# A convolution with a gated two-layer product in fp32: taps' homes, the rounds of four sums, and the engine of the weight sums

## The chip, the core and the metric

One core of a Trainium2 chip runs the whole program. The core has five engines that work side by side, each through its own queue in order: TensorE (PE, matrix products, with PEld for the loads of its weights), VectorE (DVE), ScalarE (ACT), GpSimd (POOL) and SyncE (SP, which issues DMAs). DMAs are also issued from GpSimd's queue, among them those that add to what lies at their target ("accumulating"). The metric is the device time of one execution in microseconds (us).

## The reference

Eight sequences of 4096 tokens with 192 channels pass a causal convolution of 7 taps. Its weights are a softmax over the taps, one set for each of 8 groups of channels. The result is multiplied with w_in (192 x 2048), goes through the gate h / (1 + exp(-1.702 h)), and is multiplied with w_out (2048 x 192). All in fp32.

```python
w = np.exp(weight - np.max(weight, axis=-1, keepdims=True))
w = w / (np.sum(w, axis=-1, keepdims=True) + 1e-09)
out = np.einsum('hk,bskhg->bshg', w, x_unf)      # 7 taps, causal
x = out.reshape(B * S, D)
h = x @ w_in
g = h * (1.0 / (1.0 + np.exp(-1.702 * h)))
return g @ w_out
```

## The kernel before

**Steps.** The 32768 tokens are worked in 32 steps ("big") of two parts n of 512 tokens. Step 0 (`first_step`, `second_first`) also loads the weights and makes all that later steps use. Steps 1 to 31 each have a hidden stage (`hidden`, product with w_in and the gate) and an output stage (`second`, product with w_out and the store).

**Fewer products by sums.** Both products are done with fewer matrix products than the plain way, at the price of sums of blocks. In the hidden stage 41 products (`TERMS`) of a weight block with a data block replace 48. Weight blocks 0 to 11 are w_in's own, the others are sums of these (`SUMS_W`, two sets v, in the tile `w_in_s`), made once, in step 0. Data blocks 0 to 5 are the convolution's own (`own`), 6 to 19 are sums of them: `SUMS_H`, `SUMS_M`, `SUMS_F`, `SUMS_L` and others, made for every step one step ahead. Each data block also needs its halves crossed to the other 64 partitions (`cross`, small DMAs on SP's queue, or copies of ScalarE where an engine is given). Products go to PSUM banks p0 to p3. The list `HIDDEN` says in which order the products (`mm`), the copies of banks to SBUF (`copy`, "a" is ScalarE and "v" VectorE), the `join`s of partial results on VectorE and the gates (`gelu`, ScalarE) are issued. The places k0 to k8 of copies are in `KS`: k0 is row 1 of the tile `room`, k7 and k8 are the halves of `osbs`.

**The output stage** follows the list `PLAN`. Its 78 rounds (`go`) are each one product of three small matmuls and a fourth beside them. Its operands lie in "spots": spots 0 and 1 are the two halves of `osbs`, spots 2 to 4 rows 1 to 3 of `room`, and spots 5 to 20 the blocks of `g`, the gate's output, which are also summed in place (`sum` on VectorE, `acc` by accumulating DMAs from GpSimd's queue). `osbs` has a second use: near the end of the stage results are transposed into it (`turn`; half n = 0 is spot 0, half n = 1 spot 1) and stored from it, so that it is the store's buffer.

**The convolution of later steps** runs beside both. The channels are three blocks c of 64. For steps from 3 on, ScalarE makes each tap k: it multiplies the shifted x with the tap's weight into a "home" (`tap`, `tap_home`, places in `TAP_SPOTS` and `TAP_HALVES`; a pair (i, k) there is spot i, from column block k on). Taps of blocks 0 and 1 are then added by accumulating DMAs in the order of `LATER`: under the key (c, k) stand triples (block, target, source), which are issued after tap k of block c; target 0 is the convolution's own place. Taps of block 2 are added by GpSimd (L575). There are 21 taps a step, in the order block 1, 0, 2; 18 are issued in `PLAN` and the last three, taps 4 to 6 of block 2, in the next hidden stage. `piece` issues the next of the sums `SUMS_M` (GpSimd) and crossings of the next step; `late` ends them.

**The boundary between two stages.** A hidden stage begins with the products to p1, p2 and p3, with the tap (2, 4) on ScalarE between them, then ScalarE copies p1 to k0, and the fourth product goes to p1 again.

**Step 0's end and step 1.** `second_first` makes step 0's output by sums and products of larger blocks. Its last sums are p5 and q12 (VectorE, L1015 and L1038). GpSimd makes the weight sums of set 0 and nine sums of common blocks (`make_common_1`), VectorE those of set 1. SP's queue holds, in this order, crossings of sums that GpSimd makes, the load of x for step 3 (`load_x(3)` at the end of `first_step`), and the stores of step 0, which two entries of `after_copy` issue beside the first two copies of VectorE in step 1's hidden stage. The taps of block 1 for step 2 are VectorE's (`convs_next`, L554 and L556). For step 2 the taps of block 0 are added by a tree of accumulating DMAs (`TREE`), those of block 2 by GpSimd.

Of the kernel before, what the change touches and what calls it, by code (L numbers as in the profile page):

```python
# [15 lines left out]
def kernel(  # L16
# [29 lines left out]
    nc = tc.nc  # L46
# [5 lines left out]
    P = 128  # L52
# [106 lines left out]
    TAP_HALVES = {1: ((3, 0), (1, 0), (11, 0), (2, 0), (2, 2), (11, 2)), 2: ((11, 2), (13, 0), (16, 2), (15, 2), (11, 2), (13, 0)), 3: ((5, 0), (6, 0), (12, 2), (16, 2), (15, 2), (16, 0))}  # L159
# [39 lines left out]
    def own(big):  # L199
# [35 lines left out]
        ],  # L235
        [
# [9 lines left out]
            (15, 3), (10, 5), (12, 7), (2, 13), (5, 5), (17, 11), (8, 0), (18, 10), (14, 6), (9, 14), (7, 9), (4, 4),  # L246
            (6, 19), (11, 4), (1, 14), (16, 18), (19, 16), (13, 8), (20, 17), (0, 18),
        ],
        [
            (12, 12), (18, 3), (7, 15), (3, 10), (5, 11), (15, 1), (16, 4), (13, 7), (10, 9), (19, 6), (8, 2),  # L250
            (6, 0), (14, 8), (9, 10), (17, 2), (20, 11), (2, 6), (1, 3), (11, 1), (4, 9), (0, 0),
# [181 lines left out]
    def add_up(v, dst, a, op, b, eng=vec):  # L433
        if op == "+":
            eng.tensor_add(v(dst), v(a), v(b))  # L435
        elif op == "-":
            eng.tensor_sub(v(dst), v(a), v(b))  # L437
        elif op == "n" and eng is not vec:
            eng.tensor_add(v(dst), v(a), v(b))
            eng.tensor_scalar_mul(v(dst), v(dst), -1.0)  # L440
        elif op == "n":
            vec.scalar_tensor_tensor(
                out=v(dst), in0=v(a), scalar=-1.0, in1=v(b), op0=ALU.mult, op1=ALU.subtract
            )
        else:
            eng.tensor_scalar_mul(v(dst), v(a), -1.0)

    def sums_w_in(v, eng=vec):
        for item in SUMS_W[v]:
            add_up(lambda j: w_in_s[:, j, v * P : (v + 1) * P], *item, eng=eng)  # L450
# [66 lines left out]
    def transpose_x(big, c, n=None):  # L517
# [11 lines left out]
        h if isinstance(h, int) else spot(h[0])[:, h[1] : h[1] + 2, :] for h in ((5, 2), 6, (13, 0), 7, (6, 2), (13, 2))  # L529
# [19 lines left out]
    def conv(big, c, k, ns=slice(0, 2), times=vec.tensor_scalar_mul):  # L549
# [19 lines left out]
    def tap(big, c, k):  # L569
# [4 lines left out]
        if k and c not in DMA_TAPS and big > 1:  # L574
# [108 lines left out]
    def prepare(big):  # L683
# [9 lines left out]
        yield f"done {big}", 0.0, lambda: need(f"taps {big}")  # L693
# [753 lines left out]
```

## Time and profile before

| | us |
|---|---|
| median of 3 runs | 2339.22 (2339.06 to 2341.03) |
| the profiled execution | 2337.84 |
| its span in the trace | 2336.1 |

The profile's page gives the busy time of each engine. A row of a timeline has the start and the length in us, the engine, the line of the code, the operation, the tiles written and read, and in brackets the idle time before it with what ended it. A row of the windows has the stretch, its length, the busy time of PE, PEld, DVE, ACT and POOL with the number of instructions, then the granted share of TensorE's clock, the busy share of the DMA engines and GB/s. A row of DMA issues has the number, the size of each and the median time from issue to landing.

### The profile page before, as it was taken

Reading aid. Unit: us, or ns where it says so; the run is one execution under the profiler, and the core shown is the slowest. Engines: PE = TensorE matmul, PEld = TensorE weight load, DVE = VectorE, ACT = ScalarE, POOL = GpSimd, SP = SyncE. Lnnn points to the kernel's source line nnn. Section 1 sums busy time; section 2 is a strip of 40 time slices with the busy share of each in tenths; the row PEclk is TensorE's granted clock in tenths of the full one; section 3 lists DMA queues with packets and bytes.
Section 4 is the critical chain, followed back from the end, with each engine's and each line's share of the span. In section 5 each row is a group of like instructions: output and inputs, shape, how many; then the busy total and the mean of one; then the engine's idle time right before and its main releaser. Section 6 shows DMA issues by size and latency. Waiting matters only on the chain.

```text
span 2336.1 us, 64199 instructions
## 1 busy us (share of the span) xinstructions
PE 2290.0 (98%) x25090; PEld 1331.0 (57%) x25090; DVE 2161.6 (93%) x3023; ACT 1703.4 (73%) x3331; POOL 1117.9 (48%) x1257
## 2 busy tenths in 40 slices
PE   9979999999999999999999999999999999999999
PEld 5345655555555555555566555555565666555555
DVE  8968989999999998999899999999999999999998
ACT  8557767777777777777776777777777777777745
POOL 1844544545544455545455444555444554454510
PEclk9989999999999999999999999999999999999999
DMA  9768787787987788977879877889777888777743
GB/s 201 125 144 160 153 175 145 151 158 150 175 166 153 153 160 153 177 152 144 158 148 177 160 153 151 157 162 176 155 153 152 159 169 171 153 153 136 148 98 69
DMA packets 348557, 359.30 MB, mean 154 GB/s; under 512 B 131552, under 2 KB 269152, under 8 KB 348256
## 3 DMA queue, kind: packets, MB, share of 16 engines
q0 software_dynamic: 82192, 196.32, 47.9%
q1 hardware_dynamic: 264416, 158.50, 29.7%
q8 instruction: 199, 3.26, 0.6%
q14 instruction: 102, 0.84, 0.1%
q10 hardware_dynamic: 1648, 0.39, 0.1%
HBM read 53.15 MB, written 25.17 MB: 34 GB/s over the span
## 4 chain that ended last, share of the span: by engine, by line
PE 82%; DVE 6%; DMA 5%; POOL 3%; issue 2%; ACT 1%; SPq 1%; POOLq 0%; DVEq 0%; ACTq 0%
PE slot L707 33%; PE slot L1144 24%; PE sums L1144 13%; PE sums L707 12%; DVE g L437 1%; DMA osbs<-room 1%; DVE room L437 1%; POOL conv_t L437 1%; DVE room L435 1%; SPq L99 1%; DMA g<-in_moe_w_in_dram 1%; DMA xin<-in_x_dram 1%; DMA g<-g 1%; DMA w_form<-w_form 0%; DMA room<-g 0%
## 5 line engine op out<-in xcount | busy, mean ns | idle before, releaser
L707 PE MATMUL slot<-conv_t,w_in_s 64*128 64x512 f32 x3372 | 928.8, 592 | 6.3 <-DVE room L1038 4.9
L1144 PE MATMUL slot<-g,w_form 128*32 128x256 f32 x5872 | 728.1, 380 | 1.5 <-ACT room L1169 1.1
L707 PEld LDWEIGHTS slot<-conv_t,w_in_s 64*128 64x128 f32 x3372 | 444.6, 187 | 329.1 <-issue 252.4
L437 DVE TENSOR_TENSOR g<-g 128x1024 f32<-128x1024 f32 x372 | 447.5, 1230 | 17.0 <-ACT g L826 9.3
L707 PE MATMUL sums<-conv_t,w_in_s 64*128 64x512 f32 x1284 | 426.7, 595 | 16.1 <-ACT osbs L798 15.8
L1144 PEld LDWEIGHTS slot<-g,w_form 128*32 128x32 f32 x5872 | 367.3, 110 | 120.5 <-ACT room L1169 13.1
L1144 PE MATMUL sums<-g,w_form 128*32 128x256 f32 x3800 | 428.0, 379 | 1.5 <-ACT sums L1173 1.5
L437 POOL TENSOR_TENSOR conv_t<-conv_t 128x256 f32<-128x256 f32 x310 | 273.9, 957 | 220.1 <-PE slot L707 85.6
L819 ACT ACTIVATE g<-slot 128x512 f32<-128x512 f32 x494 | 265.9, 625 | 131.9 <-PE slot L707 124.5
L573 ACT ACTIVATE g<-xt,cw 128x512 f32<-128x512 f32 x418 | 292.9, 727 | 82.5 <-DVE g L437 45.5
L1120 POOL DMA_DIRECT2D g<-g x124 | 118.3, 954 | 445.7 <-PE slot L1144 220.1
L1144 PE MATMUL slot<-g,w_out_s 128*32 128x256 f32 x4080 | 324.4, 382 | 4.3 <-DVE room L435 3.8
L575 POOL TENSOR_TENSOR conv_t<-conv_t,g 128x512 f32<-128x512 f32 x180 | 293.1, 1628 | 54.6 <-ACT g L573 52.1
L1169 ACT COPY room<-slot 32x256 f32<-32x256 f32 x434 | 158.3, 365 | 181.8 <-PE slot L1144 166.8
L1144 PEld LDWEIGHTS sums<-g,w_form 128*32 128x32 f32 x3800 | 217.5, 110 | 83.0 <-ACT room L1169 5.7
L707 PEld LDWEIGHTS sums<-conv_t,w_in_s 64*128 64x128 f32 x1284 | 181.2, 188 | 137.6 <-issue 94.3
L1144 PEld LDWEIGHTS slot<-g,w_out_s 128*32 128x32 f32 x4080 | 162.0, 110 | 96.2 <-ACT g L819 11.4
L707 PE MATMUL slot<-g,w_in_s 64*128 64x512 f32 x556 | 205.4, 594 | 3.7 <-ACT room L798 2.6
L826 ACT ACTIVATE g<-g 128x1024 f32<-128x1024 f32 x155 | 170.5, 1100 | 0.0
L1169 ACT COPY room<-sums 32x256 f32<-32x256 f32 x217 | 79.1, 365 | 97.2 <-PE sums L1144 87.1
L593 POOL DMA_DIRECT2D g<-g x116 | 118.4, 1020 | 65.2 <-ACT g L573 58.1
L1144 PE MATMUL slot<-osbs,w_form 128*32 128x256 f32 x1240 | 147.2, 381 | 0.8 <-ACT slot L1173 0.6
(245 smaller groups left out, 4030.1 us busy)
## 6 DMA issues: line engine op xcount, KB each, us to landing
g<-g POOLq DMA_DIRECT2D x124, 512.0 KB, 6.5
xin<-in_x_dram SPq DMA_DIRECT2D x240, 180.0 KB, 6.5
conv_t<-conv_t SPq DMA_DIRECT2D x664, 64.0 KB, 2.0
g<-g POOLq DMA_DIRECT2D x120, 256.0 KB, 6.5
out_dram<-osbs SPq DMA_DIRECT2D x186, 128.0 KB, 4.6
conv_t<-g POOLq DMA_DIRECT2D x89, 256.0 KB, 4.4
g<-g SPq DMA_DIRECT2D x248, 64.0 KB, 3.8
g<-room POOLq DMA_DIRECT2D x31, 512.0 KB, 5.4
```

The source lines that it names most:

```text
L99: nc.sync.dma_start(out=xin[q0 : q0 + Q, n, j:NJ, :], in_=x_v[n, p, t : t + (NJ - j) * Q, v * Q : v * Q + XW].rearrange("(j i) d -> i j d" ...
L435: eng.tensor_add(v(dst), v(a), v(b))
L437: eng.tensor_sub(v(dst), v(a), v(b))
L573: act.mul(home, conv_src(big, c, k), cw[:, c, k : k + 1])
L575: nc.gpsimd.tensor_add(dst, dst, home)
L593: nc.gpsimd.dma_start(out=out, in_=src, accum_op=ALU.add)
L707: nc.tensor.matmul(slot[h], w_in_s[halves[h], a, v * P : (v + 1) * P], src, start=first, stop=True, skip_group_check=True,)
L819: act.activation(dst[:, :, h, :], ot(bank(src, h)), AF.Gelu_apprx_sigmoid, scale=float(sign))
L826: act.activation(dst.rearrange("p o h t -> p h o t"), src, AF.Gelu_apprx_sigmoid, scale=float(sign))
L1120: nc.gpsimd.dma_start(out=spot(dst), in_=spot(a), accum_op=ALU.add)
L1144: nc.tensor.matmul(dst, w, t, start=first, stop=last, skip_group_check=True)
L1169: act.copy(to, d)
```

## The change

Four things change; PE's own order of products stays as it was, though the weight blocks have other numbers.

1. Homes. Tap 3 of block 1 moves from the first half of spot 11 (in `g`) to the second half of spot 1 (in `osbs`), and tap 4 of block 2 from the second half of spot 15 to that of spot 13. The adds follow: after tap 4 of block 1, home 3 is added into home 4, no longer home 4 into home 3; so home 4 (spot 2, row 1 of `room`) takes part in the later adds, and the last one into block 1's own place comes after tap (2, 1), no longer (2, 2). The adds behind it are issued a tap earlier too.
2. Rounds. The four sums of `SUMS_M` are issued at rounds 3, 5, 7 and 9 (before: 13, 16, 19 and 22), the crossings behind them at rounds 11 and 12 (25 and 26), `late` at 13 (27).
3. Weight sums. All are VectorE's. Three of set 1 and 24 of set 0 stand ahead of q12, one of set 0 behind it, and 18 of set 1 beside the joins of step 1's hidden stage in three groups of six. The numbers in `SUMS_W` and `TERMS` are dealt out anew. The nine common sums are VectorE's too, and two pairs of crossings become four copies of ScalarE.
4. Order around step 1. The first VectorE copy is followed by two turns and the store of half n = 1, the second by one turn. From the second join on, each join is followed by one entry of a new list `beside`: a turn, the store of half n = 0, the load of x for step 3, two late sums and a crossing; the three groups of weight sums; seven convolution taps. Step 2's taps of block 2 are added by the tree of accumulating DMAs, no longer by GpSimd, and the last forms of w_out (`add_forms(3)`) are issued in step 1's hidden stage.

```diff
-    TAP_HALVES = {1: ((3, 0), (1, 0), (11, 0), (2, 0), (2, 2), (11, 2)), 2: ((11, 2), (13, 0), (16, 2), (15, 2), (11, 2), (13, 0)), 3: ((5, 0), (6, 0), (12, 2), (16, 2), (15, 2), (16, 0))}
+    TAP_HALVES = {1: ((3, 0), (1, 0), (1, 2), (2, 0), (2, 2), (11, 2)), 2: ((11, 2), (13, 0), (16, 2), (13, 2), (11, 2), (13, 0)), 3: ((13, 0), (13, 2), (12, 2), (16, 2), (15, 2), (16, 0))}
...
     LATER = {
-        (1, 2): [(1, 2, 1)], (1, 4): [(1, 3, 4)], (1, 6): [(1, 5, 6)], (0, 0): [(1, 0, 2)], (0, 2): [(0, 1, 2)],
-        (0, 4): [(0, 3, 4)], (0, 5): [(1, 3, 5)], (0, 6): [(0, 5, 6)], (2, 0): [(0, 0, 1)], (2, 2): [(1, 0, 3)],
-        (2, 3): [(0, 3, 5)], (2, 5): [(0, 0, 3)],
+        (1, 2): [(1, 2, 1)], (1, 4): [(1, 4, 3)], (1, 6): [(1, 5, 6)], (0, 0): [(1, 0, 2)], (0, 2): [(0, 1, 2)],
+        (0, 4): [(0, 3, 4)], (0, 5): [(1, 4, 5)], (0, 6): [(0, 5, 6)], (2, 0): [(0, 0, 1)], (2, 1): [(1, 0, 4)],
+        (2, 2): [(0, 3, 5)], (2, 4): [(0, 0, 3)],
     }
...
-        if k and c not in DMA_TAPS and big > 1:
+        if k and c not in DMA_TAPS and big > 2:
             nc.gpsimd.tensor_add(dst, dst, home)
...
         for item in SUMS_F + SUMS_B_1:
-            sum_of(1, item)
-        for r in RAW_RUNS:
-            cross_run(1, *r, act.copy)
-        for r in [FIRST] + runs(*V_B):
-            cross_run(1, *r)
+            sum_of(1, item, vec)
+        for r in RAW_RUNS + [FIRST] + runs(*V_B):
+            cross_run(1, *r, None if r[1] - r[0] == 1 else act.copy)
...
             for out, x, y in banks:
                 (vec.tensor_add if op == "+" else vec.tensor_sub)(out, x, y)
+            seen_joins.append(0)
+            if beside and len(seen_joins) > 1:
+                beside.pop(0)()
...
-        sums_w_in(1 - FETCH[0], nc.gpsimd)
...
-        sums_w_in(FETCH[0])
-        sum_of(1, SUMS_ES[0], vec)
+        sums_w_in(FETCH[0], 0, 3)
+        sums_w_in(1 - FETCH[0], 0, 24)
...
         add(q12, q12, whole(c12))
+        sum_of(1, SUMS_ES[0], vec)
+        cross_run(1, V_E[0], V_E[0] + 1)
+        sums_w_in(1 - FETCH[0], 24)
+
+        def after_1():
+            turn(1, 1, blocks(p5), js)
+            turn(0, 1, blocks(q12), js)
+            store(0, 1)
...
+        def beside_1():
+            turn(0, 0, blocks(p1), js)
+            store(0, 0)
+            load_x(3)
+            for item in SUMS_ES[1:]:
+                sum_of(1, item, vec)
+            cross_run(1, V_E[0] + 1, V_S[1])
+
+        after_copy.extend([after_1, after_2])
+        beside.append(beside_1)
+        for i in range(3, len(SUMS_W[FETCH[0]]), 6):
+            beside.append(lambda i=i: sums_w_in(FETCH[0], i, i + 6))
+        beside.extend([lambda: convs_next(1)] * K)
...
-        add_forms(3)
-        end_taps()
-        load_x(3)
```

In `PLAN` the change is where the pieces stand (the start of the list, before and after):

```diff
-        ("side", 13, 16, "k0"), ("main", 1, 5, "p2", 1), ("go", 2), ("piece", 1), ("go", 2),
-        ("sum", 14, 14, "-", 18), ("main", 16, 10, "p3", 0), ("go", 2), ("sum", 7, 8, "-", 7), ("go", 2),
-        ("main", 0, 14, "p0", 1), ("go", 1), ("sum", 5, 11, "-", 19), ("go", 1), ("seed", "p4", "p2", 1), ("go", 1),
+        ("side", 13, 16, "k0"), ("main", 1, 5, "p2", 1), ("go", 2), ("piece", 1), ("go", 1), ("piece", 1), ("go", 1),
+        ("sum", 14, 14, "-", 18), ("main", 16, 10, "p3", 0), ("go", 1), ("piece", 1), ("go", 1),
+        ("sum", 7, 8, "-", 7), ("go", 1), ("piece", 1), ("go", 1), ("main", 0, 14, "p0", 1), ("go", 1),
+        ("sum", 5, 11, "-", 19), ("piece", 1), ("go", 1), ("seed", "p4", "p2", 1), ("go", 1),
+        ("seed", "k1", "p3", 1), ("piece", 1), ("go", 1), ("sum", 8, 8, "-", 16), ("seed", "p5", "k1", 1),
```

More of the change, by code (lines that the diff above doesn't have):

```diff
@@ L445, in add_up, with sums_w_in @@
         else:
[L446 to L450, printed above, removed]
+            vec.tensor_scalar_mul(v(dst), v(a), -1.0)
+    def sums_w_in(v, n0=0, n1=None):
+        for item in SUMS_W[v][n0:n1]:
+            add_up(lambda j: w_in_s[:, j, v * P : (v + 1) * P], *item)
     def load_w_out(i):
@@ L528 @@
     first_taps = [
-        h if isinstance(h, int) else spot(h[0])[:, h[1] : h[1] + 2, :] for h in ((5, 2), 6, (13, 0), 7, (6, 2), (13, 2))
+        h if isinstance(h, int) else spot(h[0])[:, h[1] : h[1] + 2, :] for h in ((5, 2), 6, (6, 2), 7, (5, 0), (6, 0))
     ]
@@ L692, in prepare @@
                 yield "", 0.7, lambda k=k: vec.tensor_add(dst, dst, tap_home(1, 0, k))
-        yield f"done {big}", 0.0, lambda: need(f"taps {big}")
+        yield f"done {big}", 0.0, lambda: (need(f"taps {big}"), end_taps())
     def prepare_taps(big):
@@ L838, in turn @@
         def turn():
-            if big + 2 < N_BIG and (not count or count.pop(0)):
+            seen.append(0)
+            if big > 1:
+                if big + 2 < N_BIG:
+                    next_turn()
+            elif len(seen) == 1:
+                add_forms(3)
+            elif len(seen) == NC:
+                while beside:
+                    beside.pop(0)()
                 next_turn()
-            if len(count) < 2:
-                count.clear()
+                need("forms")
+                held.clear()
                 while waiting:
@@ L880, in vl @@
                 next_tap()
-                convs_next(1)
-        def bring():
-            if big == 1:
-                next_turn()
-            if more:
-                fetch(big + 1, tiles[NEXT[0]])
-        waiting, count = [], [0, 1, 1, 0, 1, 1] if big == 1 else []
+        seen, seen_taps, seen_joins, waiting = [], [], [], []
+        held = [0] if big == 1 else []
         do = dict(
-            mm=mm, copy=copy, join=join, gelu=gelu, turn=turn, tap=tap, early=early, vl=vl, fetch=bring,
+            mm=mm, copy=copy, join=join, gelu=gelu, turn=turn, tap=tap, early=early, vl=vl, fetch=lambda: fetch(big + 1, tiles[NEXT[0]]) if more else None,
             over=when_more(over), ve=when_more(lambda i: sum_of(big + 1, SUMS_H[i])),
@@ L896, in hidden @@
             do[item[0]](*item[1:])
+        if big == 1:
+            for _ in range(1, NC):
+                next_turn()
     def chunk_cols(c):
@@ L1033, in second_first, with after_2 @@
         act.copy(last, whole(c21))
-        convs_next(1)
-        for item in SUMS_ES[1:]:
-            sum_of(1, item)
-        cross_run(1, V_E[0] + 1, V_S[1])
         add(q12, q12, whole(c12))
-        def out(m, n, src):
-            turn(m, n, blocks(src), js)
-            store(0, n)
-        after_copy.append(lambda: out(0, 1, q12))
-        after_copy.append(lambda: out(1, 0, last))
-    after_copy = []
+        sum_of(1, SUMS_ES[0], vec)
[5 more added lines that the diff above has]
+            store(0, 1)
+        def after_2():
+            turn(1, 0, blocks(last), js)
+        def beside_1():
[10 more added lines that the diff above has]
+        beside.extend([lambda: convs_next(1)] * K)
+    after_copy, beside = [], []
     def convs_next(n):
```

32 lines of the change are left out of this document (11 added, 21 removed), and 53 rows, old and new, of tables (PLAN, SUMS_W).

## The prediction

> **What bounds the kernel now.** I read the page first (busy time by engine), then the stages as windows, then who waited for whom, then the timelines of the two places that the change touches: step 0's end with step 1's hidden stage, and the boundary where one step's output stage hands over to the next hidden stage.
>
> ```profile
> span 2336.1 us, 64199 instructions
> PE 2290.0 (98%) x25090; PEld 1331.0 (57%) x25090; DVE 2161.6 (93%) x3023; ACT 1703.4 (73%) x3331; POOL 1117.9 (48%) x1257
> 92.30:159.10 66.80, 44.68 (x176) 28.31 (x173) 44.86 (x71) 33.23 (x61) 38.78 (x48) 0.80 0.58 116
> 625.94:662.09 36.15, 36.10 (x169) 18.61 (x165) 33.49 (x51) 28.33 (x53) 17.59 (x18) 1.00 0.67 137
> 662.09:696.89 34.80, 34.72 (x625) 21.65 (x624) 33.27 (x43) 24.96 (x52) 17.90 (x22) 1.00 0.96 181
> 696.90:1412.50 715.60, 707.22 (x7884) 410.01 (x7880) 669.29 (x922) 532.81 (x1040) 354.50 (x392) 1.00 0.81 158
> 1412.50:2262.00 849.50, 847.02 (x9459) 501.80 (x9458) 798.69 (x1101) 627.23 (x1230) 416.98 (x461) 1.00 0.79 154
> ```
>
> TensorE sets the time. Windows give length, then busy time of PE, PEld, DVE, ACT, POOL, then granted clock and DMA share. A settled step is a hidden stage of 36.2 us and an output stage of 34.8 us with PE busy in nearly all of it; the ten steps of the first long window leave 8.4 us idle, the twelve of the last 2.5. Of the 46.1 us that PE idles (2336.1 - 2290.0), 22.1 lie in step 1's hidden stage (66.8 - 44.7), which also ran at a clock of 0.80. So the settled steps hold little to win, and what they lose is lost some 29 times.
>
> **Step 1, what is removed.** Two waits of PE stand there, and the second is a queue's order.
>
> ```profile
> PE sums L707 <- ACT osbs L798: 15.8, 1, 15.8
> PE slot L707 <- DVE room L1038: 4.9, 1, 4.9
> 135.61 1.07 ACT L798 COPY osbs<-sums 128x512 f32<-128x512 f32 x2 [16.82 <-DMA out_dram<-osbs]
> 97.92 22.26 SPq L607 DMA_DIRECT2D conv_t<-conv_t  x4
> 120.22 8.77 SPq L99 DMA_DIRECT2D xin<-in_x_dram  x8
> 129.09 5.38 SPq L1073 DMA_DIRECT2D out_dram<-osbs  x6
> ```
>
> ScalarE's copy of k8 goes into the store's buffer and waits until step 0's output has left it. That store stands on SP's queue behind crossings that wait for GpSimd and behind the load of x. In the new order the store of that half follows the first VectorE copy, ahead of the load and of the late crossings; so it starts over 20 us sooner and the 15.8 us go. The 4.9 us are the sum into q12, which stood behind 21 weight sums, two turns and three taps of VectorE.
>
> **Step 1, what is added.** VectorE gets GpSimd's 25 weight sums, 24 of them ahead of q12 (27 in all there, since only three of the other set stay in that place), the nine sums of the common blocks, and 18 weight sums, an output turn, two late sums and seven taps beside the joins.
>
> ```profile
> 82.00 3.56 DVE L437 TENSOR_TENSOR g<-conv_t 128x256 f32<-128x256 f32 x4 [1.31 <-POOL conv_t L437]
> 96.86 0.41 DVE L437 TENSOR_TENSOR conv_t<-conv_t 128x256 f32<-128x256 f32 x1
> 93.05 2.13 DVE L435 TENSOR_TENSOR w_in_s<-w_in_s 128x128 f32<-128x128 f32 x5
> 78.61 8.36 POOL L437 TENSOR_TENSOR conv_t<-conv_t 128x256 f32<-128x256 f32 x8
> 108.95 1.53 DVE L556 SCALAR_TENSOR_TENSOR conv_t<-xt,cw,conv_t 128x512 f32<-128x512 f32 x2
> 102.88 0.69 DVE L1062 STREAM_TRANSPOSE osbs<-room 96x512 f32<-96x512 f32 x1
> ```
>
> One form of 128x256 took 0.89 us on VectorE while GpSimd computed and 0.41 us at 96.86; with GpSimd's sums gone, the lower end applies to more of them. At the measured 0.43 us a weight sum, 27 are 11.5 us and nine sums of 0.41 us are 3.7; against them stand 21 x 0.43 = 9.0 us that were there already, the turns and taps moved away (3.4 us) and the 1.31 us wait for GpSimd. That is +1.5 us before q12, and less where the slow forms quicken, so the 4.9 us wait between vanishing and 6.4; I take 2. Beside the joins VectorE gets 18 x 0.43 + 7 x 0.75 + 0.69 + 0.82 = 14.5 us on top of the 33.5 of a hidden stage: 48 us, more than PE's 36. So VectorE bounds this one stage: about 48 + 2 of wait + 2 of start = 52 us in place of 66.8, a gain of 15. Its ends: the two waits whole, 20.7 us, and 20.7 less the 14.5, 6 us. GpSimd's accumulating issues come earlier, as its 28 instructions of weight sums and nine of block sums leave its queue; the four copies that replace crossings load ScalarE before its taps, where it waits for VectorE anyway.
>
> [...]
>
> **The settled steps, sums issued earlier.** The four sums of GpSimd move from rounds 13 to 22 to rounds 3 to 9, the two crossings behind them from rounds 25 and 26 to 11 and 12.
>
> ```profile
> 667.79 0.86 POOL L1120 DMA_DIRECT2D g<-g  x1 [12.28 <-DMA conv_t<-conv_t]
> 668.36 2.42 POOL L437 TENSOR_TENSOR conv_t<-conv_t 128x256 f32<-128x256 f32 x3
> 675.88 0.87 POOL L1120 DMA_DIRECT2D g<-g  x1 [2.06 <-DVE g L435]
> ```
>
> They fit in the 12.28 us in which GpSimd waited; the accumulate behind them waits for PE's round 12 as before, and the next ones for VectorE. Their crossings leave earlier on SP's queue. Nothing late depends on them, so I cost this at nothing; should they be late, the accumulates would be by up to 2.42 us, of which 2.06 are idle later.
>
> **The settled steps, the homes.** The third tap of block 1 goes into the store's buffer, which the turns don't need until round 73; a tap of block 2 goes from spot 15 to spot 13. With them the order of the accumulates turns: the last add into block 1 was g (third home) at tap (2, 2); it is now room 1 (fourth home) at tap (2, 1). Room 1 is also k0, the place of ScalarE's first copy in the next hidden stage, and that copy empties bank p1 for PE's fourth product.
>
> ```profile
> 691.46 0.86 POOL L593 DMA_DIRECT2D g<-room  x1 [2.22 <-DMA room<-g]
> 694.86 1.55 POOL L593 DMA_DIRECT2D conv_t<-g  x1
> 695.46 3.58 POOL L575 TENSOR_TENSOR conv_t<-conv_t,g 128x512 f32<-128x512 f32 x2
> 698.99 0.86 POOL L593 DMA_DIRECT2D conv_t<-g  x1
> 699.33 0.72 ACT L573 ACTIVATE g<-xt,cw 128x512 f32<-128x512 f32 x1 [1.91 <-DMA g<-g]
> 700.08 1.07 ACT L798 COPY room<-sums 128x512 f32<-128x512 f32 x2
> 700.76 1.14 PE L707 MATMUL sums<-g,w_in_s 64*128 64x512 f32 x3 [1.02 <-issue]
> ACT g L573 <- DMA g<-g: 33.0, 34, 2.1
> g<-room POOLq DMA_DIRECT2D x2, 256.0 KB, 6.3
> conv_t<-g POOLq DMA_DIRECT2D x89, 256.0 KB, 4.4
> ```
>
> What goes: the tap at 699.33 waited 1.91 us for an accumulate on spot 15 (33.0 us in 34 waits), and the copy and PE behind it. What comes: k0 waits for the landing of the new last add. That add is issued after one L575 of 1.79 us, at 697.25, but not before the accumulate issued at 691.46 has landed 6.3 us later, at 697.8; 4.4 us of landing (median of its form) give 702.2. PE started 0.68 us after the copy, so 702.9 in place of 700.76: 2.1 us. A quieter step is worse:
>
> ```profile
> 1765.39 3.89 POOL L575 TENSOR_TENSOR conv_t<-conv_t,g 128x512 f32<-128x512 f32 x2
> 1768.77 1.07 ACT L798 COPY room<-slot 128x512 f32<-128x512 f32 x2
> 1769.49 1.09 PE L707 MATMUL slot<-g,w_in_s 64*128 64x512 f32 x3
> ```
>
> Half of 3.89 gives an issue at 1767.3, landing 1771.7, PE at 1772.4 in place of 1769.49: 2.9 us. Queued behind the copy are ScalarE's k5, k6 and k3, which PE needs one product later each, so they follow in time. The add isn't in the trace of before; its ends are 1.0 us (an issue two us earlier, were the queue lighter) and 3.8 (a landing of 5.3). I take 2.7, as most steps are of the second kind. It comes in hidden stages 2 to 30, 29 times: 78 us.
>
> **What the gap does to the clock.** PE would then idle some 3 us in one piece.
>
> ```profile
> 338.73 0.65 PE L1144 MATMUL slot<-g,w_out_s 128*32 128x256 f32 x3 [3.16 <-DVE room L435]
> 331.00:337.85 6.85, 4.57 (x85) 3.89 (x76) 6.78 (x7) 4.11 (x8) 6.07 (x8) 1.00 1.07 188
> 337.85:344.68 6.83, 5.95 (x38) 2.57 (x40) 5.01 (x15) 1.36 (x3) 5.20 (x5) 0.50 0.93 177
> 1109.30:1116.10 6.80, 5.26 (x88) 2.66 (x80) 2.04 (x4) 2.21 (x5) 1.71 (x2) 1.00 1.10 205
> ```
>
> One idle stretch of 3.16 us brought a granted clock of 0.50 for the next 6.83 us; 1.5 us of idling in a stretch of the same length came with none, and the long window around it has 1.00. At half clock 6.83 us lose 3.4. The stretch of before was busy to 67%, the harmless one to 77%. A gap of 3 us must lie with some 2.2 us or more inside one such stretch; of all positions of the borders that fails in (4.4 - 3.0) / 6.83, one in five. I take three in four: 0.75 x 3.4 = 2.55 us a step, 74 us. Bounds: nothing, and 3.4 each time, 99 us.
>
> **The sum.** The profiled execution took 2337.8 us, 1.7 over its span and 1.4 under the median of 2339.2. 2337.8 - 15 + 78 + 74 = 2474.8; with the 1.4, 2476 for the median.
>
> **Rivals.** First, the wait comes, the clock stays: 2339.2 - 15 + 78 = 2402. For it: gaps of 1.0 to 2.0 us stand in before without loss. Against it: the 3.16 us row, a gap of just this length. [...]
> Second, the other side: k0's wait is hidden. Then the tap no longer waits, PE gets back what it lost there, and 2339.2 - 15 - 8 = 2316 (8 of the 33.0 us, since PE idled only 8.4 + 2.5 in the two long windows, for every reason together). It decides by the landing: the quiet step's copy ran at 1768.77 with PE unhindered, and from an issue at 1767.3 that leaves 1.5 us for a transfer whose median is 4.4. Only a GpSimd queue some 3 us ahead, from the earlier sums, would do it, and the 2.22 us wait at 691.46 holds that queue back.
> Third, VectorE eats the start's gain: its 48 us come late enough that PE waits as long as before. Then 2339.2 + 78 + 74 = 2491. For it: 44.9 us of VectorE were already busy in that stage. Against: 15.8 us of PE's wait had VectorE waiting too.
>
> **How the numbers follow.** The forecast (wait and clock) has 0.6, the first rival 0.18, the second 0.12, the third 0.1. The likeliest's own range: 29 x (2.0 + 2.0) - 21 = 95 us over, 2435, to 29 x (3.4 + 3.0) - 6 = 180 over, 2520. The first rival reaches down to the low end of the wait, 2339.2 - 21 + 29 x 1.0 = 2347; so the range is 2347 to 2520 and leaves out the second rival. No change means within 0.2%, 4.7 us, about what a measurement of this kernel can tell. Faster is the second rival, 0.12 less a little: 0.11; slower the other three, 0.87; 0.02 between.
>
> **What would show it.** In the changed kernel: ScalarE's first copy into room of each hidden stage waiting 3 to 4 us on "DMA conv_t<-room", PE's fourth product waiting for it, and a granted clock below 1 in three of four hidden stages (mean clock near 0.96: 29 x 0.75 x 6.83 us at half are 3% of the span, to the 0.8% that step 1 loses now). Step 1's hidden stage near 52 us with no wait on "DMA out_dram<-osbs". Wrong, if the add lands before the copy is due, or if gaps of 3 us leave the clock at 1.00.

## The result and the profile after

The changed kernel takes 2440.4 us (median of 4 runs, 2438.9 to 2442.8) against 2340.1 us for the kernel before: a ratio of 1.0427, 95% interval 1.0409 to 1.0445. It is slower by 100 us. The prediction had said 2476, in a range of 2347 to 2520. The first rival (the wait comes, the clock stays), with 2402, is about as far off, so the number alone does not choose between the two; the profile does.

First the head of the profile's page of the changed kernel, then windows of it. The stretches answer to those of before: step 1's hidden stage, a settled hidden stage and output stage, then ten steps and twelve.

```profile
span 2438.1 us, 64102 instructions
PE 2315.9 (95%) x25090; PEld 1301.4 (53%) x25090; DVE 2155.8 (88%) x3059; ACT 1712.1 (70%) x3335; POOL 1185.2 (49%) x1218
```

```profile
91.95:152.67 60.72, 43.47 (x173) 24.14 (x169) 44.65 (x85) 34.55 (x64) 19.10 (x22) 0.86 0.67 126
640.33:680.97 40.64, 37.80 (x169) 19.30 (x165) 35.20 (x50) 28.65 (x53) 17.50 (x19) 0.96 0.58 121
680.97:715.02 34.05, 34.01 (x625) 20.06 (x624) 32.07 (x43) 24.85 (x52) 21.03 (x22) 1.00 0.99 187
715.02:1463.45 748.43, 715.53 (x7884) 414.70 (x7880) 665.76 (x920) 534.32 (x1040) 384.48 (x393) 0.98 0.77 151
1463.45:2363.73 900.28, 861.56 (x9461) 469.10 (x9457) 799.12 (x1101) 630.23 (x1230) 458.05 (x461) 0.98 0.74 145
```

The settled hidden stage went from 36.15 to 40.64 us: PE is idle 2.8 us in it, and the granted clock is 0.96 instead of 1.00. The output stage went the other way, from 34.80 to 34.05. Over ten steps PE now idles 32.9 us (748.43 - 715.53) where it idled 8.4. Step 1's hidden stage is 6.1 us shorter, which is less than half of what was forecast.

The waits of PE and ScalarE say for whom (engine and line, what ended the wait, us in all, times, the longest):

```profile
PE sums L702 <- POOL conv_t L572: 28.9, 9, 4.0
PE slot L702 <- issue: 21.6, 7, 3.3
PE slot L702 <- POOL conv_t L572: 19.1, 6, 4.0
PE sums L702 <- DMA conv_t<-conv_t: 14.9, 1, 14.9
...
ACT room L793 <- DMA conv_t<-room: 63.3, 15, 5.5
ACT room L793 <- issue: 51.0, 13, 4.9
```

ScalarE's copies wait 114 us in 28 waits, the larger part named "DMA conv_t<-room", as forecast. PE's waits behind them are put down to GpSimd's sums of L572 or to nothing, but those sums are not what PE needs. The timeline of one boundary, by GpSimd's, ScalarE's and PE's rows, shows the chain:

```profile
1009.74 0.86 POOL L590 DMA_DIRECT2D room<-room  x1 [2.66 <-DMA room<-g]
...
1013.74 2.25 POOL L572 TENSOR_TENSOR conv_t<-conv_t,g 128x512 f32<-128x512 f32 x1
1015.47 1.35 POOL L590 DMA_DIRECT2D conv_t<-room  x1
...
1020.32 1.07 ACT L793 COPY room<-sums 128x512 f32<-128x512 f32 x2 [3.88 <-DMA conv_t<-room]
1021.01 1.14 PE L702 MATMUL sums<-g,w_in_s 64*128 64x512 f32 x3 [2.99 <-POOL conv_t L572]
```

The last add into block 1 is issued at 1015.47 behind a sum of GpSimd; 4.85 us later ScalarE's copy into k0 starts, after 3.88 us of waiting; 0.69 us after that PE has its bank, after 2.99 us. That is the wait that the prediction described, in its place.

Adding up the stages of both traces (each from its first product to the first of the next stage) splits the 102.0 us between the two spans:

| | before | after | difference |
|---|---|---|---|
| up to the first product of step 1's output stage | 159.1 | 152.7 | -6.4 |
| step 1's output stage | 35.3 | 37.0 | +1.7 |
| hidden stages 2 to 31 | 1089.1 | 1215.5 | +126.4 |
| output stages 2 to 30 | 1013.6 | 993.8 | -19.8 |
| the rest | 39.0 | 39.3 | +0.3 |

In the hidden stages the records of the granted clock show 92.2 us at 0.50 (before: 2.4), so half of the difference, 44.9 us, is counted as lost to the clock; the other 81.5 us are taken for the wait.

### The profile page after: what moved, and what is told of

It reads as the page before. It is cut to its first block, busy times and chain, and to the rows that moved or that the text cites. A ratio compares the mean times of both kernels' runs of the same rounds, so it can differ in the third digit from the quotient of the medians.

```text
span 2438.1 us, 64102 instructions
## 1 busy us (share of the span) xinstructions
PE 2315.9 (95%) x25090; PEld 1301.4 (53%) x25090; DVE 2155.8 (88%) x3059; ACT 1712.1 (70%) x3335; POOL 1185.2 (49%) x1218
## 4 chain that ended last, share of the span: by engine, by line
PE 73%; POOL 9%; DVE 8%; issue 5%; DMA 3%; ACT 1%; SPq 1%; POOLq 0%; DVEq 0%; ACTq 0%
PE slot L702 32%; PE slot L1154 18%; PE sums L702 11%; PE sums L1154 11%; POOL conv_t L572 3%; DVE g L437 3%; DMA room<-g 2%; POOL g L590 2%; POOL conv_t L590 2%; POOL g L437 2%; DVE osbs L437 1%; PE slot L961 1%; DVE g L808 1%; DVE room L437 1%; SPq L99 1%
## 5 line engine op out<-in xcount | busy, mean ns | idle before, releaser
L702 PE MATMUL slot<-conv_t,w_in_s 64*128 64x512 f32 x3372 | 947.2, 609 | 2.2 <-ACT slot L793 2.0
L1154 PE MATMUL slot<-g,w_form 128*32 128x256 f32 x5872 | 715.8, 379 | 0.7 <-ACT slot L1183 0.7
L702 PEld LDWEIGHTS slot<-conv_t,w_in_s 64*128 64x128 f32 x3372 | 457.2, 194 | 341.9 <-issue 258.5
L437 POOL TENSOR_TENSOR conv_t<-conv_t 128x256 f32<-128x256 f32 x300 | 350.0, 1182 | 492.2 <-PE slot L702 170.0
L437 DVE TENSOR_TENSOR g<-g 128x1024 f32<-128x1024 f32 x372 | 503.9, 1380 | 17.0 <-ACT g L824 12.2
L702 PE MATMUL sums<-conv_t,w_in_s 64*128 64x512 f32 x1284 | 428.3, 608 | 15.2 <-DMA conv_t<-conv_t 14.9
L1154 PE MATMUL sums<-g,w_form 128*32 128x256 f32 x3800 | 422.2, 379 | 0.0
L572 POOL TENSOR_TENSOR conv_t<-conv_t,g 128x512 f32<-128x512 f32 x174 | 285.0, 1638 | 83.1 <-ACT g L570 78.6
L570 ACT ACTIVATE g<-xt,cw 128x512 f32<-128x512 f32 x389 | 270.2, 718 | 4.6
L1154 PEld LDWEIGHTS sums<-g,w_form 128*32 128x32 f32 x3800 | 210.7, 110 | 69.6
L793 ACT COPY room<-slot 128x512 f32<-128x512 f32 x216 | 121.3, 621 | 99.0 <-PE slot L702 41.8
```

What stands on the lines that cost most here:

```text
L570: act.mul(home, conv_src(big, c, k), cw[:, c, k : k + 1])
L572: nc.gpsimd.tensor_add(dst, dst, home)
L702: nc.tensor.matmul(slot[h], w_in_s[halves[h], a, v * P : (v + 1) * P], src, start=first, stop=True, skip_group_check=True,)
L793: act.copy(out, i) if sign > 0 else act.mul(out, i, -1.0)
L1154: nc.tensor.matmul(dst, w, t, start=first, stop=last, skip_group_check=True)
```

## The experiments

All ratios are to runs of the kernel before on the same chip, with 95% intervals. Sums of stages are taken as in the table above. Long lines of code are shown by their beginnings.

**1. The homes put back (homes_undone).** The rest of the change stays.

```diff
-    TAP_HALVES = {1: ((3, 0), (1, 0), (1, 2), (2, 0), (2, 2), (11, 2)), 2: ((11, 2), (13, 0), (16, 2), (13, 2), (11, 2), (13, 0)),
+    TAP_HALVES = {1: ((3, 0), (1, 0), (11, 0), (2, 0), (2, 2), (11, 2)), 2: ((11, 2), (13, 0), (16, 2), (15, 2), (11, 2), (13, 0)),
...
-        (0, 4): [(0, 3, 4)], (0, 5): [(1, 4, 5)], (0, 6): [(0, 5, 6)], (2, 0): [(0, 0, 1)], (2, 1): [(1, 0, 4)],
-        (2, 2): [(0, 3, 5)], (2, 4): [(0, 0, 3)],
+        (0, 4): [(0, 3, 4)], (0, 5): [(1, 3, 5)], (0, 6): [(0, 5, 6)], (2, 0): [(0, 0, 1)], (2, 2): [(1, 0, 3)],
+        (2, 3): [(0, 3, 5)], (2, 5): [(0, 0, 3)],
```

> Only the homes of blocks 1 and 2 and the order of their accumulates are put back to what they were; the rest of the change stays. Theory (the homes cost it all: k0's copy waits for the last add into block 1, and the gap halves the clock): the wait of ScalarE's copy into room on DMA conv_t<-room and nearly all 30 half-clock windows go, ScalarE's tap waits on DMA g<-g again; 2320 to 2336 us, so 0.2 to 0.8% faster than before by the 6 us of step 1 and perhaps the 14 us of shorter output stages. Rival (the earlier sums of GpSimd hold its queue, and the adds land late for that): stays within 10 us of 2440.

Measured: 2311.9 us, 0.9879 (0.9864 to 0.9894). The copy's wait and PE's are gone, the tap's is back:

```profile
PE sums L702 <- DMA conv_t<-conv_t: 18.3, 1, 18.3
...
ACT g L570 <- DMA g<-g: 20.5, 26, 1.8
```

Hidden stages 2 to 31 take 1080.6 us, none of it at half clock. So the homes cost some 128 us (2440.4 - 2311.9), and the rest of the change is a gain: 27 us below before, more than the expectation allowed.

**2. The homes alone (homes_alone).** The kernel before with the changed `TAP_HALVES[1]`, `TAP_HALVES[2]` and `LATER`.

> The kernel before with nothing but the new homes of blocks 1 and 2 and the new order of their accumulates. Theory: the gap ahead of the fourth product comes in the hidden stages, 29 x (3.0 wait + 1.5 half clock), about 2335 + 130 = 2440 to 2475 us. Rival (the homes cost it only together with the earlier sums): within 10 us of 2340.

Measured: 2481.6 us, 1.0610 (1.0594 to 1.0625), slightly above the upper end. Hidden stages 1233.9 us, of which 122.9 at half clock; output stages 1009.1, near those of before. From here and from experiment 1 the homes cost 128 to 143 us; the hidden stages' rise is theirs alone.

**3. Another last source (other_last).** The store's buffer stays the third home and spot 13 that of block 2; the sixth home of block 1 goes to the first half of spot 11 and collects the sums, so the last add no longer reads k0's room.

```diff
-    TAP_HALVES = {1: ((3, 0), (1, 0), (1, 2), (2, 0), (2, 2), (11, 2)),
+    TAP_HALVES = {1: ((3, 0), (1, 0), (1, 2), (2, 0), (2, 2), (11, 0)),
...
-        (1, 2): [(1, 2, 1)], (1, 4): [(1, 4, 3)], (1, 6): [(1, 5, 6)], (0, 0): [(1, 0, 2)], (0, 2): [(0, 1, 2)],
-        (0, 4): [(0, 3, 4)], (0, 5): [(1, 4, 5)], (0, 6): [(0, 5, 6)], (2, 0): [(0, 0, 1)], (2, 1): [(1, 0, 4)],
+        (1, 2): [(1, 2, 1)], (1, 4): [(1, 4, 3)], (1, 6): [(1, 6, 5)], (0, 0): [(1, 0, 2)], (0, 2): [(0, 1, 2)],
+        (0, 4): [(0, 3, 4)], (0, 5): [(1, 6, 4)], (0, 6): [(0, 5, 6)], (2, 0): [(0, 0, 1)], (2, 1): [(1, 0, 6)],
```

> The changed kernel, with the store's buffer still the third tap's home and spot 13 still that of block 2, but block 1's sixth home back in the first half of spot 11 and collecting the sums, so that the last add into block 1 reads spot 11 and not k0's room. Theory: k0 waits as in the kernel before or less, the tap of block 2 no longer waits: 2310 to 2330 us. Rival (it is the number of adds that land late, whatever they read): 2400 us or more, the wait of k0 goes on, now on another add.

Measured: 2312.3 us, 0.9888 (0.9872 to 0.9905), as the theory had it. The store's buffer as a home costs nothing that shows, and neither does a last add at tap (2, 1): what cost 128 us is that this add reads the row that ScalarE's first copy writes. PE's gap ahead of the fourth product is gone; a smaller one, mostly 0.6 to 1.2 us from start to start, stands one product later in most of the stages.

**4. Sooner and later adds (add_sooner, add_later).** The changed kernel, with the last adds of the same chain moved. They were to tell the wait's length from the clock's loss. add_sooner:

```diff
-        (0, 4): [(0, 3, 4)], (0, 5): [(1, 4, 5)], (0, 6): [(0, 5, 6)], (2, 0): [(0, 0, 1)], (2, 1): [(1, 0, 4)],
+        (0, 4): [(0, 3, 4), (1, 4, 5)], (0, 6): [(0, 5, 6)], (2, 0): [(1, 0, 4), (0, 0, 1)],
```

add_later:

```diff
-        (0, 4): [(0, 3, 4)], (0, 5): [(1, 4, 5)], (0, 6): [(0, 5, 6)], (2, 0): [(0, 0, 1)], (2, 1): [(1, 0, 4)],
-        (2, 2): [(0, 3, 5)], (2, 4): [(0, 0, 3)],
+        (0, 4): [(0, 3, 4)], (0, 5): [(1, 4, 5)], (0, 6): [(0, 5, 6)], (2, 0): [(0, 0, 1)],
+        (2, 2): [(1, 0, 4), (0, 3, 5)], (2, 4): [(0, 0, 3)],
```

> The changed kernel with the last two adds of block 1's chain issued sooner: room + room at tap (0, 4) in place of (0, 5), and the last one at (2, 0) in place of (2, 1). Homes and order of the adds stay. GpSimd then issues the last add 1 to 1.5 us sooner, so PE's gap falls from 3.7 to some 2.2 to 2.7 us from start to start. Theory (a gap of 3 us and more halves the clock, one of 2 does not): 2440 - 29 x 1.2 of wait - some 40 of half clock = 2360 to 2380 us, with few half-clock windows. Rival (any such gap halves it, or the clock is halved by something else): some 2400 to 2410 us, with as many windows as in the changed kernel.

> The changed kernel with the last add of block 1's chain issued at tap (2, 2) in place of (2, 1), behind one more sum of GpSimd. The gap grows by 1.5 to 1.9 us, to some 5.5. Theory (each gap costs its wait and one stretch of 3.4 us at half clock, whatever its length): 2440 + 29 x 1.7 = 2485 to 2495 us, the time at half clock stays near 117 us in all. Rival (a longer gap brings a longer stretch, 6.8 us as in the kernel before): 2530 to 2545 us, half clock near 215 us in all.

Measured: 2388.0 us, 1.0212 (1.0192 to 1.0232), and 2492.9 us, 1.0667 (1.0645 to 1.0688). Where a stage has the gap ahead of the fourth product, it is, from start to start, 2.82 us on the mean in add_sooner, 3.79 in the changed kernel and 4.93 in add_later; the time at half clock in all is 64, 115 and 170 us. add_sooner lies between its two theories, and add_later fell into the first one's range but not for its reason: 15 of its 29 stretches there are 6.8 us long. Length alone does not decide, since gaps of 3.2 us came with and without a loss. What does is shown by windows on a grid of 3.413 us, on which all changes of the granted clock lie in these traces (stretches at 0.50 are 3.413, 6.827 and 13.653 us long in the changed kernel). First the changed kernel, one boundary with a loss and one without:

```profile
1015.57:1018.99 3.42, 2.44 (x12) 0.77 (x8) 2.50 (x6) 0.85 (x2) 3.42 (x5) 1.00 1.01 191
1018.99:1022.40 3.41, 1.39 (x6) 0.85 (x8) 0.26 (x1) 2.08 (x5) 2.51 (x2) 1.00 1.01 178
1022.40:1025.81 3.41, 3.41 (x11) 1.66 (x9) 1.70 (x3) 2.98 (x6) 0.87 (x1) 0.50 0.83 173
1025.81:1029.23 3.42, 3.42 (x19) 1.82 (x17) 3.23 (x7) 2.48 (x5) 2.39 (x2) 1.00 0.40 69
...
493.32:496.74 3.42, 2.06 (x10) 0.58 (x6) 3.39 (x5) 0.49 (x1) 3.42 (x4) 1.00 1.06 199
496.74:500.15 3.41, 1.99 (x9) 1.24 (x11) 1.08 (x3) 2.67 (x6) 1.67 (x2) 1.00 1.01 182
500.15:503.56 3.41, 3.41 (x19) 1.80 (x17) 2.98 (x6) 3.41 (x7) 1.15 (x2) 1.00 0.96 194
```

At 1018.99 PE is busy 1.39 of 3.41 us, 41%, and the next window runs at 0.50. At 493.32 nearly as much idle time (2.78 us in two windows, against 3.00) is split evenly by a border, 60% and 58% busy, and the clock stays at 1.00. Then a long gap of add_later:

```profile
272.14:275.55 3.41, 0.00 (x0) 0.00 (x0) 0.00 (x0) 0.01 (x1) 3.11 (x3) 1.00 1.03 168
275.55:278.96 3.41, 2.73 (x7) 2.33 (x9) 0.65 (x2) 3.03 (x6) 0.87 (x1) 0.50 0.92 192
278.96:282.38 3.42, 3.42 (x11) 2.65 (x9) 1.29 (x4) 2.37 (x5) 0.00 (x0) 0.50 0.45 78
```

Here the gap reaches into the window at half clock, which is busy to 80% only, and the next one is at half clock too. The same grid explains the row of before from which the prediction worked:

```profile
331.03:334.44 3.41, 3.41 (x69) 3.25 (x64) 3.34 (x7) 2.56 (x6) 2.74 (x4) 1.00 1.10 189
334.44:337.85 3.41, 1.13 (x21) 0.62 (x13) 3.41 (x1) 1.52 (x3) 3.33 (x5) 1.00 1.04 187
337.85:341.27 3.42, 2.54 (x24) 1.19 (x28) 2.82 (x9) 0.00 (x0) 3.42 (x4) 0.50 0.86 175
341.27:344.68 3.41, 3.41 (x18) 1.38 (x12) 2.19 (x6) 1.36 (x3) 1.78 (x2) 0.50 0.99 179
```

What the prediction read as one stretch of 6.85 us with 67% of work is a full window and one that is busy to 33%. The 6.83 us at half clock behind it are two windows, of which the first is busy to 74% only.

Counted over all windows from 160 us on to 60 us before the end in five traces (the changed kernel, homes_alone, add_sooner, add_later, cross_first): of 127 windows at full clock in which PE was busy under 50%, 126 were followed by one at half; of some 2970 above 50%, none. A window at half clock was followed by another in all 19 that were busy under 80%, in 6 of 10 between 80 and 90%, and in none of 122 above. The half and the 80 to 90% are what these five traces show; no run here was made to look for the exact limits.

**5. The order of the output stage alone (rounds_alone).** The kernel before with nothing but the changed `PLAN`.

> The kernel before with nothing but the new output-stage order: the four sums of GpSimd and their crossings at rounds 3 to 12. The prediction cost this at nothing. Theory after the first runs (the changed kernel with the homes put back has output stages of 34.45 us on the mean against 34.95 of before, and the homes alone leave them at 34.80): it is this order that shortens them, by 0.4 to 0.5 us each: 2318 to 2328 us. Rival (they are shorter because a tap no longer waits or GpSimd is freed at the start): 2335 to 2343 us, output stages at 34.9.

Measured: 2310.7 us, 0.9890 (0.9876 to 0.9905), a larger gain than expected. Output stages 2 to 30 take 991.1 us (34.2 each), 22.5 less than in before; hidden stages take 1083.6, 5.5 less. So the part that the prediction cost at nothing is worth 27 us. The gain of the rewritten step 1 does not show in the whole: homes_undone, which has both, took 2311.9. Its output stages took 999.2 us for the same order, and why they took 8 us more was not tested.

What changes beside PE is a sum of VectorE. In the timeline of the kernel before, of one output stage, and in that of rounds_alone for the same step:

```profile
875.21 5.88 DVE L437 TENSOR_TENSOR g<-g 128x1024 f32<-128x1024 f32 x5
881.01 3.65 DVE L437 TENSOR_TENSOR room<-g 128x1024 f32<-128x1024 f32 x1
881.15 2.42 POOL L437 TENSOR_TENSOR conv_t<-conv_t 128x256 f32<-128x256 f32 x3
```

```profile
864.48 6.83 POOL L437 TENSOR_TENSOR conv_t<-conv_t 128x256 f32<-128x256 f32 x4 [5.77 <-PE slot L707]
865.61 8.04 DVE L437 TENSOR_TENSOR g<-g 128x1024 f32<-128x1024 f32 x5
...
873.57 1.22 DVE L437 TENSOR_TENSOR room<-g 128x1024 f32<-128x1024 f32 x1
```

The same sum takes 1.22 us when GpSimd is quiet and 3.65 beside three of its sums: longer by 2.43, and these three take 2.42. VectorE lost as much time as all three took. By the starts of the rows VectorE's sum was the first of the two, at 881.01 against 881.15, and it was still the one that took longer.

In the new order GpSimd's four sums meet the five sums from 865.61 on. These take 8.04 us, where five took 5.88 in before, and GpSimd's take 1.7 us each (6.83 for four), where they took 0.8 (2.42 for three). So VectorE loses 2.16 us there, nearly as much as the 2.43 of before. What the new order changes is above all the place at which VectorE is late.

**6. The sums without their crossings (crossings_late).** As rounds_alone, but the two crossings behind the sums and `late` stay at rounds 25 to 27. The diff is against the kernel before.

```diff
-        ("side", 13, 16, "k0"), ("main", 1, 5, "p2", 1), ("go", 2), ("piece", 1), ("go", 2),
+        ("side", 13, 16, "k0"), ("main", 1, 5, "p2", 1), ("go", 2), ("piece", 1), ("go", 1), ("piece", 1), ("go", 1),
...
-        ("sum", 7, 8, "-", 7), ("go", 2),
+        ("sum", 7, 8, "-", 7), ("go", 1), ("piece", 1), ("go", 1),
...
-        ("acc", 14, 13), ("main", 18, 0, "p2", 0), ("go", 1), ("piece", 1), ("go", 2), ("sum", 6, 8, "-", 6),
+        ("acc", 14, 13), ("main", 18, 0, "p2", 0), ("go", 3), ("sum", 6, 8, "-", 6),
...
```

> The kernel before with GpSimd's four sums at rounds 3 to 9, as in the changed one, but their crossings left at rounds 25 and 26. Theory (the sums themselves, beside VectorE's sum of 128x1024 from g into room, made that one take 3.4 us in place of 1.2, and PE waited behind it later in the stage): 2306 to 2316 us, as with the whole new order (2310.7), and that sum at 1.2 us. Rival (the crossings, sent 14 rounds sooner, clear SP's queue and DMA for later transfers): 2330 to 2340 us.

Measured: 2313.1 us, 0.9887 (0.9872 to 0.9902); the sum into `room` takes 1.22 us, output stages 994.5 us. So it is the place of the four sums, not that of the crossings. How the 2.4 us that VectorE is late become 0.5 (median) to 0.8 us (mean) of PE in each stage is only argued: counted from a stage's first product, PE's records fall behind by 0.1 to 0.2 us at a time between the 320th and the 600th of 624 matmuls in the kernel before, where banks are emptied or sums are due, and no longer in rounds_alone, which loses 0.24 us once, at the 128th, mostly behind VectorE.

**7. Step 1's late sums first (cross_first).** The changed kernel with `beside_1` reordered. In this order the late sums write over block p1 before its turn has read it, so that part of step 0's output is wrong; the work is the same.

```diff
         def beside_1():
-            turn(0, 0, blocks(p1), js)
-            store(0, 0)
-            load_x(3)
             for item in SUMS_ES[1:]:
                 sum_of(1, item, vec)
             cross_run(1, V_E[0] + 1, V_S[1])
+            turn(0, 0, blocks(p1), js)
+            store(0, 0)
+            load_x(3)
```

> The changed kernel with step 1's last late sums and their crossing put ahead of the output turn, the store and the load of x, instead of behind them. Theory: PE's 14.95 us wait on DMA conv_t<-conv_t in step 1's hidden stage goes for the most part, VectorE bounds that stage at some 48 us: 6 to 13 us less than the changed kernel. Rival (VectorE's work beside the joins was what ended it, the crossing hidden behind): within 3 us of the changed kernel, with the wait on VectorE in its place.

Measured: 2436.2 us, 1.0418 (1.0402 to 1.0433), so 4.2 us less than the changed kernel by the medians, with intervals that overlap, and short of the expectation. By the traces the end of step 1's output stage comes 7.3 us sooner. PE's 14.9 us wait is gone, and a wait of 6.5 us on VectorE's join has come, as the rival had it. The cause of the old wait stands in the changed kernel's timeline, by rows of VectorE, SP's queue and PE:

```profile
94.60 1.69 SPq L604 DMA_DIRECT2D conv_t<-conv_t  x2
97.21 11.82 SPq L1083 DMA_DIRECT2D out_dram<-osbs  x6
105.60 0.71 DVE L437 TENSOR_TENSOR conv_t<-conv_t 128x256 f32<-128x256 f32 x2
109.09 12.11 SPq L99 DMA_DIRECT2D xin<-in_x_dram  x8
121.30 10.33 SPq L604 DMA_DIRECT2D conv_t<-conv_t  x4
128.28 2.08 PE L702 MATMUL sums<-conv_t,w_in_s 64*128 64x512 f32 x4 [14.95 <-DMA conv_t<-conv_t]
```

The two late sums are ready at 106.3, but their crossing stands on SP's queue behind the six parts of the two stores and the eight of the load, and is issued at 121.30.

**8. Versions that beat both kernels.** Each takes the crossing ahead of the store and of the load, but behind the turn of p1, whose block the late sums write over:

```diff
             turn(0, 0, blocks(p1), js)
-            store(0, 0)
-            load_x(3)
             for item in SUMS_ES[1:]:
                 sum_of(1, item, vec)
             cross_run(1, V_E[0] + 1, V_S[1])
+            store(0, 0)
+            load_x(3)
```

With the homes of other_last (both), with those of before (undone_cross), and with those of before but block 2's tap in spot 13 (spot13_cross):

> The changed kernel with the sixth home in the first half of spot 11, collecting the sums, and in step 1 the late sums and their crossing right behind the output turn, ahead of the store and of the load of x. Theory: the gains add up, 2312 less 4 to 7 us of step 1's 15 us wait on DMA conv_t<-conv_t: 2305 to 2308 us. Rival (the store now goes so late that ScalarE's copy into its buffer waits for it again, as before): 2310 us or more with a wait on DMA out_dram<-osbs.

> The changed kernel with the homes and adds of before, and in step 1 the late sums and their crossing ahead of the store and of the load of x. Theory: 2312 less 4 to 8 us for the shorter step 1: 2303 to 2308 us, the same as the version with the sixth home in spot 11 (2303.8), whose hidden stages are 0.2 us longer. Rival (step 1's gain is given back in its output stage): 2310 to 2314 us.

> As the version with the homes of before and the crossing ahead, but with the tap of block 2 in spot 13 in place of spot 15 (the one part of the new homes that takes a wait away). Theory: ScalarE's tap no longer waits on DMA g<-g (20.5 us in 26 waits), but PE's gaps there are small (0.66 us against 0.43 of the ordinary distance), so 0 to 7 us less than without it: 2296 to 2308 us. Rival (spot 13 is free later than it is needed): 2310 us or more, with a new wait of ScalarE's tap.

Measured: both 2303.8 us, 0.9855 (0.9834 to 0.9877); undone_cross 2303.7, 0.9849 (0.9833 to 0.9865); spot13_cross 2298.3, 0.9824 (0.9808 to 0.9839). SP's queue in undone_cross, and the product that needs the crossing:

```profile
97.25 1.55 SPq L1083 DMA_DIRECT2D out_dram<-osbs  x3
105.27 2.62 SPq L604 DMA_DIRECT2D conv_t<-conv_t  x2
107.93 4.16 SPq L1083 DMA_DIRECT2D out_dram<-osbs  x3
112.13 10.79 SPq L99 DMA_DIRECT2D xin<-in_x_dram  x8
112.77 1.13 PE L702 MATMUL sums<-conv_t,w_in_s 64*128 64x512 f32 x4 [0.96 <-DMA conv_t<-conv_t]
```

The crossing leaves at 105.27 and PE waits 1 us for it. The first output stage starts at 141.9 us, against 154.5 in homes_undone, of which a part is the clock: homes_undone has 20.5 us at half clock from 114.2 on, the larger part of it within its 18.3 us wait and the end behind it; undone_cross has none there. ScalarE's copy into the store's buffer waits 2.3 us for the store there, and 6.3 us in both, where PE waits 3.3 us for that copy: the wait that the rival of the run "both" named is there, but the median of both stays below that of other_last. Block 2's tap in spot 13 gains another 5.4 us by the medians, while the two intervals still overlap; ScalarE's wait of 20.9 us on "DMA g<-g" falls to 1.0, and hidden stages 2 to 31 from 1081.5 us to 1074.6. So this is the one part of the new homes that seems to pay. The page of spot13_cross begins:

```profile
span 2293.0 us, 64156 instructions
PE 2265.9 (99%) x25090; PEld 1361.6 (59%) x25090; DVE 2142.2 (93%) x3059; ACT 1718.0 (75%) x3335; POOL 1179.1 (51%) x1218
```

## Why the prediction was right, and where it was not

The sign, the place and the main mechanism were right: the last add into block 1, k0's copy, the fourth product, the clock. The sum 2476 was 36 us too high, and that it came so near is in part luck: the clock's term and the four sums were out by 29 and 20 us in one direction, step 1 and the wait by 10 and 4 in the other. By its terms, from the profiles:

| term | predicted | measured |
|---|---|---|
| step 1 (up to the end of its output stage) | -15 | -4.7 |
| the wait in the hidden stages | +78 | +81.5 |
| half clock in the hidden stages | +74 | +44.9 |
| the four sums' rounds, in output stages | 0 | -19.8 |

1. **The wait.** 29 x 2.7 us were forecast; 28 of 29 boundaries have it. The working from the issue behind one sum of GpSimd, a landing and 0.68 us to PE came out as in the rows at 1015.47 to 1021.01. The size was a little low. Where the gap is, it is 3.79 us from start to start, 3.4 more than the ordinary distance of 0.43; the landing was taken from another form, with 4.4 us, and that of this form has a median of 5.0. The 81.5 us of the table are lower than 28 x 3.4, in the main because hidden stages got shorter elsewhere: they take 1080.6 us in homes_undone against 1089.1 in before. Experiments 1 to 3 show that this add's source makes the wait, and not the store's buffer or spot 13 as homes.
2. **The clock.** The mechanism was right, the size was not. The step that failed is "At half clock 6.83 us lose 3.4": one row of before, a stretch of 6.83 us, was taken for the unit. The unit is 3.413 us, that row was two of them (experiment 4), and in the changed kernel 25 of 26 stretches in hidden stages are one unit: 1.7 us counted as lost in each, half of 3.413. That they would come in "three in four" steps was too low: 26 of the 28 gaps have one. By the count of experiment 4 a unit with more than some 1.7 us of idling was followed by half clock in 126 of 127 cases; with that a gap of 3 us escapes when a border splits it nearly in half, as at 493.32. The other of the two gaps without a stretch is the one case of 127: it has 2.01 us in the window from 1165.75 on, and the clock stays at 1.00. The mean clock came out at 0.976, where 0.96 was forecast.
3. **Step 1.** The step that failed is the sentence that the store goes "ahead of the load and of the late crossings; so it starts over 20 us sooner and the 15.8 us go". They did go, and so did the 4.9 us. But the order was read for the store only. The crossing that now stands behind store and load feeds PE too, and PE waits 14.95 us for it. The bound of 48 us of VectorE did not decide: it was busy 44.65 of 60.72 us.
4. **The weight sums** cost less than the 0.43 us each that were taken:

```profile
88.26 1.02 DVE L435 TENSOR_TENSOR w_in_s<-w_in_s 128x128 f32<-128x128 f32 x4
...
93.52 0.68 DVE L1030 TENSOR_TENSOR room<-room,slot 96x512 f32<-96x512 f32 x1
```

   In VectorE's timeline of the changed kernel these four take 0.26 us each. All 27 take 6.6 us, from 86.97 to the sum into q12 at 93.52, where 11.5 were forecast, and PE does not wait for that sum. The 0.43 us were measured in before at 93.05, where GpSimd made weight sums too; in the changed kernel GpSimd's queue holds only issues of DMAs in that time, as these rows of before and after show:

```profile
93.40 1.63 POOL L437 TENSOR_TENSOR w_in_s<-w_in_s 128x128 f32<-128x128 f32 x3
```

```profile
88.57 3.68 POOL L595 DMA_DIRECT2D g<-g  x3
```

   So 0.26 us, the rate without GpSimd's sums, would have been the figure to take; what it gained was lost in the wait of point 3.
5. **The four sums.** "Nothing late depends on them, so I cost this at nothing" failed. Their own results are not late, but VectorE loses time while they run (2.43 us in the rows of before, 2.16 in those of rounds_alone), and rounds 13 to 22 were the worse place for it. Experiments 5 and 6 show 25 to 27 us; why a delay of VectorE costs PE less at the new place is argued and not shown.
6. **The rivals.** That the clock would stay (2402) is refuted by 92 us of half clock in the hidden stages; that the wait would be hidden (2316), by 28 gaps. That step 1's gain would be eaten (2491) came two thirds true, but by SP's queue and not by VectorE.

The tap that waited for spot 15 was priced at 8 us within the second rival; spot13_cross shows 5.4.

## What to carry to other kernels

When a step in a chain of adds changes its source or its place, ask who writes that place next: the buffer that the change was about was harmless, and a row that only became the last source in passing cost 128 us. When a transfer is moved up in a queue, list every other entry that it passes and who waits for it (PE waited 14.95 us for one here), and when work of GpSimd is moved, look at which VectorE instruction runs beside it at both places (one sum took 3.65 us here in place of 1.22). An idle gap of PE had a second price through the clock here, 44.9 us by the count above beside 81.5 of wait, and it depended on how the gap fell into windows of 3.413 us: of some 2970 windows at full clock with PE idle for less than half of them none was followed by half clock, of 127 with more idle time 126 were.

## What the runs showed of the hardware

- The granted clock changed on a grid of 3.413 us. Of 127 windows at full clock with PE busy under half of the time, 126 were followed by one at half clock, of some 2970 with PE busy for more than that none. Of the windows among them with 40 to 50% of work it was 15 of 16. A window at half clock was followed by another in all 19 cases with PE busy under 80% and in none of 122 above 90% (five traces, experiment 4).
- One sum of VectorE took longer by the whole of three sums of GpSimd beside it: 3.65 us (881.01 in before) against 1.22 (873.57 in rounds_alone), with 2.42 us of GpSimd. Where sums of both engines meet one by one (from 865.61 on in rounds_alone), both get longer: five of VectorE take 8.04 us in place of 5.88, and GpSimd's 1.7 us each in place of 0.8.
- Accumulating DMAs of 256 KB between places of SBUF took several us each from issue to landing (medians: conv_t<-g 4.4 in before, conv_t<-room 5.0 and room<-room 5.2 in the changed kernel), and a chain of them adds up: the add issued at 1009.74 had waited 2.66 us for the one ahead of it, and the last one, issued at 1015.47, released ScalarE 4.85 us later.
